# Routed experts: outputs turned by VectorE and scattered as quarters, inputs gathered as rows and passed through DRAM

## Chip, cores and metric

One core of one Trainium2 chip. The metric is the device time of one execution in microseconds; times below are of the kernel before the change.

## What is computed

```python
def reference(q, k, v, moe_w_group, moe_w_expert, moe_w1, moe_w2):
    x = attention(q, k, v)                   # [4608 tokens, 512]: local window plus 4x pooled attention
    g_logits = x @ w_group                   # 4 groups: argmax and its softmax value g_w
    for g in range(4):
        e_logits = x[mask_g] @ w_expert[g]   # 4 experts of the group: argmax and its softmax value e_w
        for e in range(4):
            h = np.maximum(xg[mask_e] @ w1[g, e], 0.0)     # 512 -> 1024
            ye = h @ w2[g, e]                              # 1024 -> 512
            out[tok_idx] = (g_w * e_w)[:, None] * ye
```

Everything is float32. Each of the 4608 tokens goes to one of 16 experts; its output row is the expert's result times the token's share g_w * e_w.

## The kernel before, in words

The first 230 us or so are attention: an order written out by hand (a string of steps, ORDER) over 16 units of two heads and two batches. Its results go to DRAM as rows of 512 floats, `xd` [4608, 512], written by `store_x` (line 455) in pieces of 512 B per row from the ACT queue. The router finds each token's expert and its share, and writes the shares to DRAM, 16 equal floats a token, `xw`, in `weight`. For each expert it makes a list of token numbers.

The experts follow. One expert is taken early and finished late, while attention still runs out; the other 15 are sorted by their count of tokens, and rank r has room for CAPS[r] of them (416, 384, 368, 352, ... 256, 256). Each rank r below 14 is one turn of `main`, that is one call of `ranked` (line 1157) with four experts: `pv`, the rank before, whose outputs are stored; `st`, the rank computed; `nx`, the next, whose weights are loaded and whose inputs are prepared; and `nn`, the one after, whose inputs are gathered. A turn stands in the program twice where the rank's count may be 20 smaller (`arm`): a branch picks one of the two.

A turn has ten steps. Steps 0 to 7 each compute a hidden block of 128 of the 1024 rows (`hidden`, line 961 the matmuls: 12 of C columns, since every float32 product is made of three float32r ones), then ScalarE takes the relu (line 965) and VectorE the rest that the rounding left (line 966). Steps 2 to 9 each project one hidden block into four accumulators (`project`, line 1012, 12 matmuls), which hold the output transposed: 128 of the 512 columns by C tokens. Weights come in four chunks (`weights_in`, line 876: 512 KB of w1 and 512 KB of w2, issued by SP into two raw buffers), and are split into a rounded part (ScalarE, line 881) and a rest (VectorE, line 882). A chunk waits until the one before the last is split and its raw buffer free. SP issues in order.

Outputs: at step 0 `drain` (line 1014) copies the four accumulators to `yt`, two by VectorE and two by ScalarE. At steps 1, 2 and 3 `store` (line 1025) turns one tile of 128 tokens with four transposes on TensorE (line 1034), scales it by the tokens' shares (ScalarE for even tiles, line 1039, VectorE for odd ones, line 1037) into `yo`, and GpSimd scatters the rows to `out` by an indirect DMA (line 1040). Ranks 1, 13 and 14 have a multiple of 128 tokens; they are computed in rows and have no drain and no turning.

Inputs of ranks 2 to 14: `xd` is read as quarters of a row, [4 * 4608, 128]. One indirect DMA of GpSimd gathers, for 32 tokens, quarter q to partitions 32q to 32q + 31 (`gather_quarters`, line 922, by `fetch`, line 905): with C tokens that is C / 32 of them per rank, spread over steps 1, 3, 5 and 7, the indices made by VectorE (`quarter_list`, line 826). Three more gather the shares. One turn later VectorE turns blocks of 32 by 32 (`turn_quarters`, line 935, steps 4 to 7), after which the columns stand in an order that the weights `w1q`, permuted on the host, have too; ScalarE and VectorE split them (lines 941, 942). Ranks 0 and 1 and the early and late expert gather rows instead and turn them on TensorE (`turn_in`, line 948).

Of the kernel before, what the change touches and what calls it, by code (L numbers as in the profile page):

```python
# [29 lines left out]
NTOK = B * S  # L30
LINE = 16
DM = H * D
# [13 lines left out]
SWITCHED = (0, *range(3, 13))  # L46

# [451 lines left out]
class Router:  # L499
# [7 lines left out]
    def __init__(self, ctx, tc, wg, we, cp, idf, xw):  # L507
        nc = self.nc = tc.nc
        self.idf, self.xw, self.cp = idf, xw, cp
# [142 lines left out]
    def weight(self, bp):  # L652
# [14 lines left out]
        nc.sync.dma_start(out=self.xw[G * P * bp : G * P * bp + G * P].rearrange("(g p) f -> p g f", p=P), in_=cw)  # L667
# [28 lines left out]
class Experts:  # L696
# [9 lines left out]
    def __init__(self, tc, cp, w1, w2, out, xd, xw, idf, R, ps, psd, px, lgp):  # L706
# [3 lines left out]
        self.w1, self.w2, self.out, self.xd, self.xw, self.idf = w1, w2, out, xd, xw, idf  # L710
# [29 lines left out]
        self.quad = f([P, 2], "quad")  # L740

    def numbers(self):
# [3 lines left out]
        for q in range(4):  # L746
            for i in range(2):
                nc.gpsimd.memset(self.quad[32 * q : 32 * q + 32, i : i + 1], float(q - 4 + 4 * i))
# [68 lines left out]
    def quarter_lists(self, c):  # L817

        n = NE - 3
        pt = self.psum([P, n, 4], "ql")  # L820
        self.nc.tensor.matmul(pt, self.four[:, c].rearrange("p q i -> p (q i)"), self.rv[:, 2 : n + 2], start=True, stop=True, skip_group_check=True)
        self.nc.vector.tensor_copy(self.qf[:, c], pt)

    def quarter_list(self, st, c):
        r = st["r"]
        self.nc.vector.tensor_scalar(
            out=self.qi[r % 2][:, c], in0=self.qf[:, c, r - 2], scalar1=self.quad[:, 0:1], scalar2=self.quad[:, 1:2], op0=ALU.add, op1=ALU.max
# [15 lines left out]
    def pools(self, ctx):  # L843
# [4 lines left out]
        self.xq = [xp.tile([P, 16, P], F32, name=f"xq{i}") for i in range(2)]  # L848
        self.qf = xp.tile([P, 4, NE - 3, 4], F32, name="qf")
        self.qi = [xp.tile([P, 4, 4], I32, name=f"qi{i}") for i in range(2)]  # L850
        self.four = xp.tile([P, 4, 4, 32], F32, name="four")
        self.xt = [xp.tile([P, 13, 32], F32, name=f"xt{i}") for i in range(2)]
        self.xs = [[xp.tile([P, 4, CAPS[i]], F32R, name=f"x{n}{i}") for n in "hl"] for i in range(2)]
        self.shares = [xp.tile([P, 4, LINE], F32, name=f"shares{i}") for i in range(4)]
        self.yt = xp.tile([P, 4, CAPS[0]], F32, name="yt")
# [28 lines left out]
    def gather(self, st, rows=NTOK):  # L884
# [4 lines left out]
        else:  # L889
            st["xh"] = self.xp.tile([P, 4, C], F32R, tag=n + "xh", name="xh")  # L890
            st["xl"] = self.xp.tile([P, 4, C], F32R, tag=n + "xl", name="xl")
            st["cw"] = self.xp.tile([P, C // P, LINE], F32, tag=n + "cw", name="cw")
        self.tiles(st)
        for t, (c, m, *_, w) in enumerate(st["xg"]):
            if "r" in st:
                xg = self.xq[st["r"] % 2].rearrange("p b c -> p (b c)")[:, DM * t : DM * t + DM]
            else:
                xg = self.xp.tile([P, DM], F32, tag=f"{n}xg{t}", name=f"xg{t}")
            self.fetch(xg[:w], self.xd[0:rows], st["gi"][:w, t : t + 1])
            st["xg"][t] = (c, m, xg, *st["xg"][t][3:])  # L900
        if "r" not in st:
            self.gather_shares(st, rows)

    def fetch(self, out, in_, index):
        self.nc.gpsimd.indirect_dma_start(  # L905
            out=out, out_offset=None, in_=in_, in_offset=bass.IndirectOffsetOnAxis(ap=index, axis=0), bounds_check=in_.shape[0] - 1, oob_is_err=False
        )

    def tiles(self, st):

        C = st["C"]
        cw = self.shares[st["r"] % 4] if "r" in st else st["cw"]
# [9 lines left out]
    def gather_quarters(self, st, blocks):  # L922

        C, r = st["C"], st["r"]
        if "xg" not in st:
            self.tiles(st)
# [651 lines left out]
```

## Time and profile before

| | us |
|---|---|
| median of 3 runs (693.62 to 693.8) | 693.62 |
| the profiled execution | 694.55 |
| its span, first to last instruction | 692.8 |
| TensorE busy in the span | 654.5 |
| VectorE, ScalarE, GpSimd busy | 486.7, 382.5, 427.1 |

The profile is of one execution; its span is 1.75 us shorter than that execution's own time, and that is 0.93 us above the median of the runs. TensorE's instructions overlap in the records, so the start of one matmul to the start of the next is what one costs in a stream, and the busy time of a group of them can be less than their number times the mean.

### The profile page before, as it was taken

The numbers are of one execution on the slowest core, as the hardware profiler recorded it, in microseconds if no ns is written. First come the engines' busy times: TensorE is split into PE (matmuls) and PEld (weight loads), VectorE is DVE, ScalarE is ACT, GpSimd is POOL, SyncE is SP. The second block draws the span as 40 slices with busy tenths as digits, with TensorE's granted clock in tenths as the row PEclk, the third lists the DMA queues.
The fourth block names the chain that finished last, engine by engine and source line by source line (L and its number), as shares of the span: only waits on it lengthen the run. The fifth ranks groups of instructions, "written<-read, shape, count | busy, mean of one in ns | idle before, by whom it ended". The sixth has DMA issues, their size and how long they took to land. (4 is left out here: it accounts for less than half of the span.)

```text
span 692.8 us, 18020 instructions
## 1 busy us (share of the span) xinstructions
PE 654.5 (94%) x6874; PEld 585.5 (85%) x6875; DVE 486.7 (70%) x937; ACT 382.5 (55%) x835; POOL 427.1 (62%) x457
## 2 busy tenths in 40 slices
PE   7798997998997999999999999999999999999996
PEld 4575775776765887999899999999999999999995
DVE  6987887988895686556456666667676767677751
ACT  8786765775773536344344454545555556556541
POOL 7957655668452745777564746667767677667411
PEclk9999999999999999999999999999999999999999
DMA  8798799889869537945464747677576686677720
GB/s 312 198 282 278 238 292 271 235 232 272 234 204 280 167 123 228 293 118 186 146 200 132 220 131 229 185 208 208 176 228 210 181 254 204 190 228 244 230 70 27
DMA packets 108450, 144.51 MB, mean 209 GB/s; under 512 B 25168, under 2 KB 77120, under 8 KB 108336
## 3 DMA queue, kind: packets, MB, share of 16 engines
q1 hardware_dynamic: 81120, 113.47, 54.2%
q0 software_dynamic: 9696, 20.72, 9.2%
q10 hardware_dynamic: 17520, 8.85, 4.6%
q8 instruction: 66, 1.08, 0.7%
q14 instruction: 48, 0.39, 0.2%
HBM read 121.47 MB, written 22.51 MB: 208 GB/s over the span
## 5 line engine op out<-in xcount | busy, mean ns | idle before, releaser
L905 POOL DMA_INDIRECT xq<-xd,qi x126 | 155.4, 1233 | 70.2 <-issue 36.9
L961 PE MATMUL ph<-xh,w1h 128*128 128x256 f32 (+13 forms) x512 | 153.9, 301 | 1.5 <-issue 1.0
L961 PE MATMUL ph<-xh,w1l 128*128 128x256 f32 (+13 forms) x512 | 152.3, 298 | 0.0
L961 PE MATMUL ph<-xl,w1h 128*128 128x256 f32 (+13 forms) x512 | 152.2, 298 | 0.0
L965 ACT ACTIVATE hh<-ph 128x256 fp32r<-128x256 f32 (+13 forms) x128 | 53.1, 416 | 172.7 <-PE ph L961 142.4
L966 DVE SCALAR_TENSOR_TENSOR hl<-ph,hh 128x256 fp32r<-128x256 f32 (+13 forms) x128 | 59.0, 463 | 99.3 <-ACT hh L965 64.3
L1012 PE MATMUL y<-hh,w2h 128*128 128x396 f32 (+11 forms) x384 | 117.4, 306 | 0.0
L1012 PE MATMUL y<-hl,w2h 128*128 128x396 f32 (+11 forms) x384 | 115.1, 300 | 0.0
L1012 PE MATMUL y<-hh,w2l 128*128 128x396 f32 (+11 forms) x384 | 115.0, 300 | 0.0
L1040 POOL DMA_INDIRECT out_dram<-yo,oi x47 | 57.9, 1231 | 79.2 <-ACT yo L1039 35.1
L961 PEld LDWEIGHTS ph<-xh,w1h 128*128 128x128 f32 x512 | 96.2, 188 | 3.3 <-issue 1.7
L961 PEld LDWEIGHTS ph<-xl,w1h 128*128 128x128 f32 x512 | 96.2, 188 | 0.9
L961 PEld LDWEIGHTS ph<-xh,w1l 128*128 128x128 f32 x512 | 96.2, 188 | 0.1
L882 DVE TENSOR_TENSOR w2l<-raww,w2h 128x1024 fp32r<-128x1024 f32 x61 | 74.4, 1222 | 22.5 <-ACT w2h L881 13.1
L882 DVE TENSOR_TENSOR w1l<-raww,w1h 128x1024 fp32r<-128x1024 f32 x61 | 74.4, 1219 | 13.2 <-ACT w1h L881 9.7
L1012 PEld LDWEIGHTS y<-hh,w2h 128*128 128x128 f32 x384 | 72.3, 188 | 0.6 <-DVE yo L1037 0.3
L1012 PEld LDWEIGHTS y<-hl,w2h 128*128 128x128 f32 x384 | 72.4, 189 | 0.1
L1012 PEld LDWEIGHTS y<-hh,w2l 128*128 128x128 f32 x384 | 72.3, 188 | 0.0
L881 ACT ACTIVATE w1h<-raww 128x1024 fp32r<-128x1024 f32 x64 | 67.5, 1055 | 4.1 <-DMA raww<-in_moe_w_dram 3.1
L881 ACT ACTIVATE w2h<-raww 128x1024 fp32r<-128x1024 f32 x64 | 67.2, 1051 | 1.2 <-DMA raww<-in_moe_w_dram 0.7
L905 POOL DMA_INDIRECT shares<-xw,gi x44 | 45.4, 1032 | 13.4 <-issue 13.4
L448 PE MATMUL b_x<-vw,pt 126*32 126x128 f32 x1152 | 39.9, 275 | 7.0 <-issue 3.7
(248 smaller groups left out, 1313.8 us busy)
## 6 DMA issues: line engine op xcount, KB each, us to landing
raww<-in_moe_w_dram SPq DMA_DIRECT2D x76, 512.0 KB
raww<-in_w1q_dram SPq DMA_DIRECT2D x52, 512.0 KB
vw<-in_vw_dram SPq DMA_DIRECT2D x32, 378.0 KB
kt<-in_k_dram SPq DMA_DIRECT2D x16, 576.0 KB
qT<-in_q_dram SPq DMA_DIRECT2D x16, 576.0 KB
xd<-x ACTq DMA_DIRECT2D x15, 576.0 KB
vs<-in_vm_dram SPq DMA_DIRECT2D x16, 512.0 KB
vw<-odd SPq DMA_DIRECT2D x16, 144.0 KB
```

Source lines behind the costliest of these rows:

```text
L448: self.nc.tensor.matmul(pt[32 * j : 32 * j + 32, t], self.of("pt", u)[:ROWS, 32 * lin : 32 * lin + 32], self.windows(u)[:ROWS, :, lin], st ...
L881: self.nc.scalar.activation(hi, raw, AF.Copy)
L882: eng.tensor_tensor(out=lo, in0=raw, in1=hi.bitcast(F32), op=ALU.subtract)
L905: self.nc.gpsimd.indirect_dma_start(out=out, out_offset=None, in_=in_, in_offset=bass.IndirectOffsetOnAxis(ap=index, axis=0), bounds_check ...
L961: nc.tensor.matmul(ph, a[:, k, cs], st[b][:, k, 0:C], start=(n == 0), stop=(n == 11))
L965: nc.scalar.activation(hh, ph, AF.Relu)
L966: nc.vector.scalar_tensor_tensor(out=hl, in0=ph, scalar=0.0, in1=hh.bitcast(F32), op0=ALU.max, op1=ALU.subtract)
L1012: nc.tensor.matmul(y, a[:, f % 2, cs], b, start=(f == 0 and n == 0), stop=(f == 7 and n == 2))
L1040: i = nc.gpsimd.indirect_dma_start(out=self.out, out_offset=bass.IndirectOffsetOnAxis(ap=oi, axis=0), in_=yo[:m], in_offset=None, bounds_c ...
```

## The change

- Turned ranks are 2 to 12 (`TURNED`). Their `drain` has no copies: VectorE transposes each accumulator in blocks of 32 by 32 straight into `yt` (two buffers), where 32 tokens by four quarters of a row then stand as 128 partitions of 128 floats. `store` is not called for them; at steps 1, 3, 5 and 8 VectorE makes the target indices of quarters, and `store_quarters` scatters up to three blocks, each by one indirect DMA of 128 pieces of 512 B. The order of columns that this needs comes from `w2q`, permuted on the host and read in place of w2.
- Since nothing scales the outputs any more, the inputs are scaled (relu and both products pass a factor through that is above zero). Rows in DRAM become 528 floats, the last 16 the share (`ROW`); `xw` and its gathers go. For rank `nn`, step 0 gathers whole rows (one indirect DMA per 128 tokens), steps 3, 4 and 5 scale a tile each on ScalarE, and at step 6 SP writes them to a DRAM buffer `xl` (two DMAs, `lay_down`). At step 0 of the next turn SP reads them back as quarters (four DMAs, `pick_up`) into one `xq`, where there were two.
- Ranks 0 and 1 and the early and late expert keep the shares of their gathered rows in a small tile (`keep_shares`, ScalarE) and scale at the end, as before. The last input tile of `turn_in` is 32, 64, 96 or 128 wide.

```diff
+ROW = DM + LINE
+TURNED = range(2, 13)
+SCATTER = (1, 3, 5, 8)
+SCALED = {3: (0,), 4: (1,), 5: (2,)}
...
     def targets(self, lo, hi, oi):
...
-        V.scalar_tensor_tensor(out=oi, in0=self.rv[:, lo:hi], scalar=-1.0, in1=self.none[:, lo:hi], op0=ALU.add, op1=ALU.add)
+        V.scalar_tensor_tensor(out=self.none[:, lo:hi], in0=self.rv[:, lo:hi], scalar=-1.0, in1=self.none[:, lo:hi], op0=ALU.add, op1=ALU.add)
+        V.tensor_copy(oi, self.none[:, lo:hi])
...
-        src2 = self.w2[ds(e, 1)].rearrange("a (k p) f -> p (a k) f", p=P)[:, 2 * c : 2 * c + 2, :]
+        src2 = self.w2[st.get("r", 0) in TURNED][ds(e, 1)].rearrange("a (k p) f -> p (a k) f", p=P)[:, 2 * c : 2 * c + 2, :]
...
+    def scale(self, st, t):
+        *_, xg, _, _, w = st["xg"][t]
+        self.nc.scalar.activation(xg[:w, 0:DM], xg[:w, 0:DM], AF.Copy, scale=xg[:w, DM : DM + 1])
+
+    def lay_down(self, st):
+
+        n = st["C"] // P
+        for t, m, w in ((0, n, P), (n, len(st["xg"]), st["xg"][-1][-1])):
+            if t < m:
+                self.nc.sync.dma_start(
+                    out=self.xl[st["r"] % 2].rearrange("(t p) c -> p t c", p=P)[:w, t:m], in_=self.xg[st["r"] % 2][:w, t:m, 0:DM]
+                )
+
+    def pick_up(self, st, q):
+        nb = (st["C"] + 31) // 32
+        self.nc.sync.dma_start(
+            out=self.xq[32 * q : 32 * q + 32, 0:nb], in_=self.xl[st["r"] % 2].rearrange("(b i) c -> i b c", i=32)[:, 0:nb, P * q : P * q + P]
+        )
...
     def drain(self, st):
...
+        if r in TURNED:
+            nb = (st["C"] + 31) // 32
+            yt = st["yt"] = self.yt[r % 2][:, 0 : 4 * P * 3].rearrange("p (b d j) -> p b d j", d=4, j=32)
+            for d in range(4):
+                nc.vector.transpose(yt[:, 0:nb, d], self.ys[d][:, 0 : 32 * nb].rearrange("p (b i) -> p b i", i=32))
+            return
...
+    def store_quarters(self, st, b):
+        t, c = divmod(b, 4)
+        if 32 * b < st["C"]:
+            self.scatter(self.out.rearrange("n (q c) -> (n q) c", q=4), self.qo[st["r"] % 2][:, c, t : t + 1], st["yt"][:, b].rearrange("p d j -> p (d j)"))
...
     def ranked(self, pv, st, nx, nn, hint):
...
                 self.drain(pv)
+                if st["r"] < 2:
+                    self.keep_shares(st)
                 if first:
                     self.gather(nx)
+                if nn:
+                    self.tiles(nn)
+                    for t in range(len(nn["xg"])):
+                        self.fetch(nn, t)
...
-            t = f if rows else f - 1
-            if t in range(len(pv["xg"])):
-                self.store(pv, t)
+            if turned:
+                if f in SCATTER:
+                    self.quarter_list(pv, SCATTER.index(f))
+                    for t in range(3):
+                        self.store_quarters(pv, 4 * t + SCATTER.index(f))
+            else:
+                t = f if rows else f - 1
+                if t in range(len(pv["xg"])):
+                    self.store(pv, t)
...
-            elif first and f in (2, 4):
-                self.gather_shares(st, lo=f - 2, hi=f)
-            elif first and f in (6, 8):
-                self.gather_shares(nx, lo=f - 6, hi=f - 4)
-            if nn and f in (1, 3, 5, 7):
-                self.quarter_list(nn, f // 2)
-                self.gather_quarters(nn, range(f // 2, 16, 4))
-            if nn and f == 8 + first:
-                self.gather_shares(nn)
             if f > 1:
                 self.project(st, f - 2)
+            for t in SCALED.get(f, ()):
+                if nn and t < len(nn["xg"]):
+                    self.scale(nn, t)
...
             if f in (1, 3, 5):
                 self.weights_in(nx, e, (f + 1) // 2)
+            if not first and f == 0:
+                for q in range(4):
+                    self.pick_up(nx, q)
+            if nn and f == 6:
+                self.lay_down(nn)
...
-    xd = dram.tile([NTOK, DM], F32, name="xd")
-    xw = dram.tile([NTOK, LINE], F32, name="xw")
+    xd = dram.tile([NTOK, ROW], F32, name="xd")
```

## Rows read from the trace of the kernel before

**Rows 1.** The page: busy time and share of the engines; TensorE in 40 slices.

```profile
PE 654.5 (94%) x6874; PEld 585.5 (85%) x6875; DVE 486.7 (70%) x937; ACT 382.5 (55%) x835; POOL 427.1 (62%) x457
...
PE   7798997998997999999999999999999999999996
```

**Rows 2.** TensorE's waits, 308 to 690 us: total, times, longest.

```profile
PE ph L961 <- issue: 1.0, 1, 1.0
PE ph L961 <- ACT yo L1039: 0.5, 1, 0.5
```

**Rows 3.** Windows: PE, PEld, DVE, ACT, POOL busy; clock; DMA share; GB/s.

```profile
437.02:464.85 27.83, 27.83 (x207) 27.80 (x205) 18.77 (x31) 14.39 (x24) 18.57 (x17) 1.00 0.67 200
...
618.14:641.16 23.02, 23.02 (x207) 22.96 (x205) 17.46 (x33) 13.72 (x25) 16.21 (x14) 1.00 0.72 219
...
100.00:125.00 25.00, 20.11 (x388) 14.60 (x387) 20.72 (x45) 15.08 (x50) 15.01 (x17) 1.00 0.96 287
```

**Rows 4.** TensorE's timeline around one store, turn of rank 5: start, duration.

```profile
437.02 0.30 PE L961 MATMUL ph<-xh,w1h 128*128 128x300 f32 x1
...
440.30 0.60 PE L1034 MATMUL yr<-idf,yt 128*128 128x128 f32 x4
440.66 0.39 PE L961 MATMUL ph<-xh,w1h 128*128 128x300 f32 x1
440.88 0.30 PE L961 MATMUL ph<-xl,w1h 128*128 128x300 f32 x1
441.01 0.30 PE L961 MATMUL ph<-xh,w1l 128*128 128x300 f32 x1
```

**Rows 5.** Instructions on the tiles yr and yt: ns min/median/max.

```profile
L1034 PE MATMUL yr<-idf,yt x148: 270/272/274, 313.0 to 649.3; 128*128 128x128 f32 x100, 128*32 128x128 f32 x8, 128*112 128x128 f32 x4, 128*96 128x128 f32 x4
L1039 ACT ACTIVATE yo<-yr,shares x24: 678/683/689, 314.2 to 650.2; 128x512 f32<-128x512 f32 x13, 112x512 f32<-112x512 f32 x1, 96x512 f32<-96x512 f32 x1, 80x512 f32<-80x512 f32 x1
L1037 DVE TENSOR_SCALAR yo<-yr,shares x13: 729/743/745, 317.5 to 648.9; 128x512 f32<-128x512 f32 x12, 32x512 f32<-32x512 f32 x1
...
L1023 ACT ACTIVATE yt<-y x24: 391/428/517, 307.4 to 641.0; 128x416 f32<-128x416 f32 x2, 128x368 f32<-128x368 f32 x2, 128x352 f32<-128x352 f32 x2, 128x336 f32<-128x336 f32 x2
L1021 DVE COPY yt<-y x24: 416/479/592, 307.9 to 641.8; 128x416 f32<-128x416 f32 x2, 128x368 f32<-128x368 f32 x2, 128x352 f32<-128x352 f32 x2, 128x336 f32<-128x336 f32 x2
```

**Rows 6.** Instructions on the tile xt: ns min/median/max.

```profile
L941 ACT ACTIVATE xh<-xt x68: 272/442/548, 223.4 to 664.1; 128x256 fp32r<-128x256 f32 x12, 128x128 fp32r<-128x128 f32 x4, 128x416 fp32r<-128x416 f32 x4, 128x384 fp32r<-128x384 f32 x4
...
L935 DVE STREAM_TRANSPOSE xt<-xq x52: 434/500/575, 326.6 to 663.3; 128x320 f32<-128x320 f32 x16, 128x288 f32<-128x288 f32 x16, 128x352 f32<-128x352 f32 x8, 128x256 f32<-128x256 f32 x8
```

**Rows 7.** The page's costliest groups: busy, mean ns, idle before.

```profile
L905 POOL DMA_INDIRECT xq<-xd,qi x126 | 155.4, 1233 | 70.2 <-issue 36.9
...
L1040 POOL DMA_INDIRECT out_dram<-yo,oi x47 | 57.9, 1231 | 79.2 <-ACT yo L1039 35.1
...
L881 ACT ACTIVATE w1h<-raww 128x1024 fp32r<-128x1024 f32 x64 | 67.5, 1055 | 4.1 <-DMA raww<-in_moe_w_dram 3.1
```

**Rows 8.** SP's timeline, turn of rank 5: start, duration.

```profile
442.16 0.37 SPq L876 DMA_DIRECT2D raww<-in_w1q_dram  x1
```

**Rows 9.** Waits of SP, 300 to 690 us: total, times, longest.

```profile
SPq L876 <- DVE hl L966: 97.8, 32, 7.6
```

**Rows 10.** Windows of 1 us after that issue; columns as in rows 3.

```profile
442.20:443.20 1.00, 1.00 (x10) 1.00 (x9) 0.69 (x3) 1.00 (x3) 0.89 (x1) 1.00 0.00 0
...
444.20:445.20 1.00, 1.00 (x10) 1.00 (x9) 1.00 (x4) 0.04 (x1) 0.95 (x1) 1.00 1.07 340
```

**Rows 11.** ScalarE's timeline, turn of rank 5: start, duration.

```profile
450.40 1.05 ACT L881 ACTIVATE w1h<-raww 128x1024 fp32r<-128x1024 f32 x1
```

**Rows 12.** DMA queues in the turn of rank 12: packets, MB, share.

```profile
q1 hardware_dynamic: 2923, 3.93, 57.0%
q0 software_dynamic: 512, 1.05, 13.8%
```

**Rows 13.** The page: the ACT queue of DMAs over the span.

```profile
q10 hardware_dynamic: 17520, 8.85, 4.6%
```

More of the change, by code (lines that the diff above doesn't have):

```diff
@@ L30 @@
 NTOK = B * S
+DM = H * D
 LINE = 16
-DM = H * D
+ROW = DM + LINE
 F = 1024
@@ L746, in numbers @@
         for q in range(4):
-            for i in range(2):
-                nc.gpsimd.memset(self.quad[32 * q : 32 * q + 32, i : i + 1], float(q - 4 + 4 * i))
+            nc.gpsimd.memset(self.quad[32 * q : 32 * q + 32], float(q))
         for r, c in enumerate(CAPS):
@@ L817, in quarter_lists @@
     def quarter_lists(self, c):
-        n = NE - 3
-        pt = self.psum([P, n, 4], "ql")
-        self.nc.tensor.matmul(pt, self.four[:, c].rearrange("p q i -> p (q i)"), self.rv[:, 2 : n + 2], start=True, stop=True, skip_group_check=True)
+        lo, hi = TURNED.start, TURNED.stop
+        pt = self.psum([P, hi - lo, 3], "ql")
+        self.nc.tensor.matmul(pt, self.four[:, c].rearrange("p q i -> p (q i)"), self.none[:, lo:hi, 0:3], start=True, stop=True, skip_group_check=True)
         self.nc.vector.tensor_copy(self.qf[:, c], pt)
@@ L826, in quarter_list @@
         self.nc.vector.tensor_scalar(
-            out=self.qi[r % 2][:, c], in0=self.qf[:, c, r - 2], scalar1=self.quad[:, 0:1], scalar2=self.quad[:, 1:2], op0=ALU.add, op1=ALU.max
+            out=self.qo[r % 2][:, c], in0=self.qf[:, c, r - TURNED.start], scalar1=self.quad, scalar2=None, op0=ALU.add
         )
@@ L891, in gather @@
             st["xl"] = self.xp.tile([P, 4, C], F32R, tag=n + "xl", name="xl")
-            st["cw"] = self.xp.tile([P, C // P, LINE], F32, tag=n + "cw", name="cw")
+            st["tiles"] = self.xp.tile([P, C // P, ROW], F32, tag=n + "xg", name="xg")
         self.tiles(st)
[L894 to L907, printed above, removed]
+        for t in range(len(st["xg"])):
+            self.fetch(st, t, rows)
     def tiles(self, st):
-        C = st["C"]
-        cw = self.shares[st["r"] % 4] if "r" in st else st["cw"]
+        C, r = st["C"], st.get("r")
+        xg = st["tiles"] if r is None else self.xg[r % 2]
         st["xg"] = []
@@ L915, in tiles @@
             m = min(P, C - P * t)
-            st["xg"].append((P * t, m, None, st["oi"][:m, t : t + 1], cw[:, t], P if m <= P // 2 else m))
-    def gather_shares(self, st, rows=NTOK, lo=0, hi=4):
-        for t, (*_, cw, _) in list(enumerate(st["xg"]))[lo:hi]:
-            self.fetch(cw, self.xw[0:rows], st["gi"][:, t : t + 1])
[L922 to L926, printed above, removed]
-        for b in blocks:
-            t, c = divmod(b, 4)
-            if 32 * b < C:
-                self.fetch(self.xq[r % 2][:, b], self.xd.rearrange("n (q c) -> (n q) c", q=4), self.qi[r % 2][:, c, t : t + 1])
+            share = None if r is not None and r > 1 else self.shares(st)[:m, t : t + 1]
@@ new lines, in tiles, with fetch, shares @@
+            st["xg"].append((P * t, m, xg[:, t], st["oi"][:m, t : t + 1], share, 32 * ((m + 31) // 32)))
+    def fetch(self, st, t, rows=NTOK):
+        *_, xg, _, _, w = st["xg"][t]
+        self.nc.gpsimd.indirect_dma_start(
+            out=xg[:w], out_offset=None, in_=self.xd[0:rows], in_offset=bass.IndirectOffsetOnAxis(ap=st["gi"][:w, t : t + 1], axis=0),
+            bounds_check=rows - 1, oob_is_err=False,
+        )
+    def shares(self, st):
+        i = st.get("r", 2 + (st["C"] == P))
+        return self.share[:, 4 * i : 4 * i + 4]
@@ L949, in turn_in @@
         self.split(st["xh"][:, k], st["xl"][:, k], pt[:, : st["C"]])
+        if k == 3 and "r" not in st:
+            self.keep_shares(st)
     def hidden(self, st, f):
@@ L1287, in tables @@
     def tables(self, dram):
+        self.xl = [dram.tile([3 * P, DM], F32, name=f"xl{i}") for i in range(2)]
         self.t_units = dram.tile([UNITS, 2], I32, name="t_units")
```

63 lines of the change are left out of this document (38 added, 25 removed).

## The prediction

> **What bounds the kernel now.** I read the page first: TensorE is busy 94% of the span, and its slices stand at 9 from the fourteenth to the last but one; beside its own weight loads, which overlap, no other engine is above 70% [rows 1]. That says which engine, not which stage, and a busy TensorE need not be one that gains from less work. So I read its waits from the first rank's store to the end: two, 1.5 us in all, in 380 us [rows 2]. Nothing is late for TensorE there; whatever leaves its instruction stream shortens the run until something else becomes late. The windows by turn say how far off that is: in the turn of rank 5 (437.02 to 464.85) VectorE has 18.77 of 27.83 us busy, ScalarE 14.39, GpSimd 18.57, the DMA engines 0.67; in the turn of rank 12 (618.14 to 641.16), one of the shortest, 17.46, 13.72 and 16.21 of 23.02 us, DMA 0.72 [rows 3]. The attention stage before 230 us is another case: from 100 to 125 us the DMA share is 0.96 and TensorE is busy 20.11 of 25 us [rows 3].
>
> **What leaves TensorE.** A store of ranks 0 and 2 to 12 turns four 128-column blocks on TensorE. The timeline of one store shows the price: 24 matmuls of the hidden layer start between 437.02 and 440.30, 0.137 apart; at 440.30 the four transposes start where the 25th would have; that matmul begins at 440.66, its successor at 440.88, the third at 441.01 [rows 4]. Undisturbed the third would have begun at 440.57, so a store displaces 0.44 us. The instruction's own 272 ns would say 1.09 for four, since their ends overlap; the shift of what follows is what the end of the run sees. The trace has 148 such transposes [rows 5]: 12 ranks, 16 of rank 0 (four tiles), and 11 times 12 of ranks 2 to 12. These 132 go: 33 stores by 0.44 is **14.5 us**. Bounds: 0.36 for the four starts alone gives 11.9, and 0.46 with one more disturbed start gives 15.2. Smaller: the last tile of rank 0's input is turned 32 wide instead of 128, 4 instructions by at most 0.09, so 0 to 0.4 us; I take 0.2.
>
> **What VectorE gets.** Per turned rank two copies of 0.479 and one scaling of 0.743 go [rows 5], and four transposes of 32 by 32 blocks come, from PSUM. Nearest row: the same instruction from SBUF, median 0.50 [rows 6]; the copy from PSUM, 0.479, is no dearer, so I take 0.50 and bound it by 0.45 and 1.0. That is 2.0 for 1.7, so 17.8 of about 21.7 us busy in the turn of rank 12: covered. The place matters more: all four stand at the head of the turn, ahead of the first relu residue, and the accumulators they empty are needed by the first projection, three hidden blocks later (36 matmuls: 4.9 us at the 0.137 of 300 columns [rows 4], 4.0 at the 244 of rank 12). Each starts as its quarter of the last projection ends, so they are done 1 to 1.5 us into the turn; even at 1.0 each they are done by 3.3. Nothing is late. The index arithmetic (one small operation at four steps) stays, at steps 1, 3, 5, 8 instead of 1, 3, 5, 7.
>
> The Trainium skill speaks against this part: its page "VectorE: DVE Perf Modes", section "Rules for kernel authors", gives a 128 by 128 transpose to TensorE when PSUM will do as the destination. By that rule the 33 stores would stay and the time with them, near 693.6; the rows say that here it is TensorE that has no time left, and the sum goes by them.
>
> **ScalarE.** Two drains (0.428) and two scalings (0.683) go per turned rank [rows 5], 2.2 us; three scalings of the gathered rows come for ranks 2 to 14. Between the 0.683 from PSUM and half of the 1.055 for 1024 columns from SBUF [rows 7] I take 0.6, so 1.8. The tightest step is 5: relu and input split, near 0.44 each [rows 6], scaling 0.6 and weight split 1.05 are 2.5 of the 2.7 us that a hidden block and a projection take at rank 12; covered, and steps 8 and 9 have little.
>
> **GpSimd.** Ten gathers of quarters (1.233), three of shares and three scatters (1.231) per rank [rows 7] become three row gathers and ten quarter scatters. With as many indices each, I price them alike, at 1.25 and a quarter between two: 16 issues become 13, 19.5 us instead of 24, in turns of 21 to 34. The tightest cover of the change is here. Behind the two or three scatters of step 8, which wait for VectorE's index operation, stand the next turn's row gathers: with 1 us for that wait, the first is issued 5.5 us after step 8 began, 2.8 us into the next turn, and with 2.5 us to land (an estimate: the weight chunk below, twice as large, takes about 3) is there at 5.3; ScalarE reads it behind the relu of step 3, at 6.8 or later. Each further tile comes 1.5 us later and is read a step of 2.7 us later. No cost; without that 1.5 us, ScalarE's relu is late next.
>
> **The DRAM trip: SP and the DMA engines.** Two DMAs lay a rank's rows down and four pick them up, six more issues of 0.37 on SP [rows 8], 2.2 us a turn; SP now waits 97.8 us for VectorE's relu residues alone, behind which the weight buffers come free [rows 9], and that idle time hides them. Order on SP: weight chunk 3, lay-down (waits for the scaling of step 5), next chunk 0 (freed at steps 6 and 7), the pick-ups (wait for the lay-down to land and for the last turning of step 7), chunk 1. Half a chunk, 512 KB, issued at 442.16 [rows 8] moves nothing until 443.2, then up to 340 GB/s [rows 10]: some 3 us to land. The lay-down has steps 6 and 7, 5.4 us or more, before the pick-ups are reached. Behind them chunk 1 is queued: issued at 442.16, first read by ScalarE at 450.40 [rows 11], 5 us to spare. The picked-up blocks are turned at step 4, some 13 us after. Cost 0 with that cover; without it, the first thing late is chunk 1.
>
> The engines' own time: in the turn of rank 12 the 3.93 MB of the hardware queue take 57.0% of 23.02 us, 13.1 us, so 3.34 us per MB; the indirect queue 13.8%, 3.2 [rows 12]. Lay-down and pick-up of 256 rows of 2 KB are 1.05 MB more, 3.5 us; the share gathers that go, and 64 B per row that come, nearly cancel. So 16.6 becomes 20.1 of 21.6 us, share **0.93**, under the 0.96 that the attention stage held for 25 us [rows 3]; at rank 5 18.6 becomes 22.8 of 26.5, 0.86. I take 0 and bound it at 6 us (below).
>
> **Attention stage.** The rows in DRAM are 2112 B apart, not 2048, under the same 512 B writes; the ACT queue's time is 4.6% of the span, 32 us [rows 13]. No row shows the new pitch: a fifth dearer is 6 us of DMA time among 230, of which at most 1.5 would show. I take 0.3. The shares of the early and late expert come with their rows, three gathers fewer on GpSimd, with no TensorE wait behind them: 0 to 0.5 back, taken as 0.
>
> **Sum.** The profiled execution took 694.55 (span 692.8 and 1.75 around it), the median of the runs is 693.62, 0.93 lower. 694.55 - 14.5 - 0.2 + 0.3 = 680.15; less 0.93, **679.2**.
>
> **Rivals.**
> A, the forecast: the turns of ranks 3 to 13 shrink by 1.3 us each and TensorE still waits for nothing. For it: two waits in 380 us, and every cover above is 1.5 us or more. 676.5 to 681.
>
> B, the DMA engines become the bound in the late turns. For: 0.93 by the sum, in a stream that arrives in bursts, with 4 us more of engine time in a turn that is 1.3 shorter. Against: at a share of 1.07 they moved 340 GB/s [rows 10], and turn 12 needs 3.93, 1.05 and 1.05 MB in 21.6 us, 279 GB/s. If a share of 0.9 is all that bursts allow, the turns of ranks 8 to 13 take 22.3 instead of 21.7, 0.6 to 1 us each: 3.6 to 6, so 683 to 685. The Trainium skill bears on this: "DMA: Bandwidth & Descriptors", section "Rules for kernel authors", wants at least 1 MiB per DMA and calls anything under 64 KB mostly overhead. The pick-ups are 128 to 176 KB each, between the two; at twice the price per byte they would add 1.8 us to the 20.1, which is this rival. No row here shows such a DMA.
>
> C, slower than before: the pick-ups hold SP. They wait in SP's queue for a write to DRAM to be confirmed, and chunk 1 stands behind them. It decides once that wait lasts beyond about 10 us into a turn (5 us of spare at chunk 1, 5 more in the relu that waits behind it on ScalarE); each microsecond beyond stalls TensorE by one, in 13 turns. To lose all that is gained takes 14.4 / 13 = 1.1 us per turn; at 2 us it is 705. For: two trips in one queue are new here. Against: 3 us landings seen, and a lay-down issued some 9 us before the turn begins.
>
> D, hidden anyway: something unseen paces the turns at their old length, 693 to 694. For: SP spends most of the time waiting for VectorE [rows 9], so the weight stream moves at VectorE's pace. Against: the turns are as long as their matmuls and stores: 192 by 0.137 and three by 0.44 are 27.6, of the 27.83 that rank 5 took.
>
> **Chances.** A 0.73, B 0.16, C 0.07, D 0.04. Faster by over 0.2% (1.4 us, about what a measurement of this kernel can tell from no change) takes A and B, 0.89; D is the same, 0.04; C is slower, 0.07. The range holds A and most of B: 676 to 686; it leaves C and D out.
>
> **What would show it.** Right: 16 transposes from line store, none in ranks 2 to 12; the turn of rank 12 at 21.7 us and that of rank 5 at 26.5; TensorE waits from 300 us on still about 1.5 us; block transposes from PSUM near 0.50; DMA share 0.85 to 0.95 late. Wrong by B: late turns longer than 192 matmuls, weight splits waiting for a weight DMA. Wrong by C: SP waiting for the lay-down past the start of a turn, the same splits late from rank 1 on. Wrong by the attention term: the gaps of TensorE before 230 us grow by more than 1 us.

## The result, and the profile after

The changed kernel takes 684.82 us (median, 683.76 to 686.88), the kernel before beside it 693.62: a ratio of 0.988, interval 0.985 to 0.991. That is faster, inside the range, and 5.6 us above the predicted 679.2. Two later series of the unedited kernel, both on the chip that the record numbers 2, gave 0.990 (0.986 to 0.993) and 0.998 (0.994 to 1.002), more below.

From the page of the changed kernel, its span, busy times and DMA queues (packets, MB, share of 16 engines):

```profile
span 683.7 us, 17694 instructions
PE 642.7 (94%) x6743; PEld 573.8 (84%) x6743; DVE 489.3 (72%) x942; ACT 384.5 (56%) x833; POOL 353.7 (52%) x394
...
q1 hardware_dynamic: 102496, 129.99, 65.7%
q0 software_dynamic: 7952, 20.47, 10.1%
q10 hardware_dynamic: 17520, 8.85, 4.8%
q8 instruction: 66, 1.08, 0.7%
```

The span fell by 9.1 us. TensorE has 11.8 us less work than in [rows 1], so it is idle longer than before, the reverse of what was forecast. GpSimd lost 73 us, which moved nothing by itself. Queue q8, which the prediction did not read, brings instructions: 66 packets of 16 KB.

Now the same kernel's TensorE waits from 300 us to 690 us, which answer to [rows 2]:

```profile
PE ph L979 <- issue: 3.4, 4, 1.3
PE y L1030 <- issue: 0.5, 1, 0.5
```

Before, 1.5 us in two waits; now 3.9 in five. None names an engine or a DMA: "issue" is time in which TensorE waited for nothing that the profile shows. Three of the five stand at the start of a turn, the other two, 0.54 each, inside the turns of ranks 10 and 12.

Third, the windows of the turns of ranks 5 and 12 (length, busy us of PE, PEld, DVE, ACT, POOL, clock, DMA share, GB/s), to set against [rows 3]:

```profile
434.40:461.00 26.60, 26.60 (x195) 26.60 (x193) 18.77 (x33) 14.43 (x23) 17.11 (x15) 1.00 0.95 260
610.62:633.19 22.57, 22.03 (x195) 21.85 (x194) 16.98 (x33) 13.25 (x22) 13.42 (x12) 1.00 0.94 266
```

Rank 5 came out as forecast (26.5), with a DMA share of 0.95 and TensorE never idle. Rank 12 is 0.9 over its 21.7, half a microsecond of it idle. So a full DMA share is not what costs, and the late turns are where the time stayed. Turn lengths, from the start of one turn's first matmul of the hidden layer to the next one's; the last column is a version that comes up below:

| turn of rank | before | after | after, code moved by 8 KB |
|---|---|---|---|
| 4 | 29.18 | 27.74 | 28.40 |
| 5 | 27.83 | 26.59 | 26.59 |
| 6 | 26.86 | 25.72 | 25.72 |
| 8 | 25.60 | 25.83 | 24.39 |
| 10 | 24.45 | 25.39 | 23.05 |
| 12 | 23.02 | 22.57 | 21.78 |
| 3 to 13 | 286.65 | 276.95 | 272.02 |

Early turns lost 1.1 to 1.4 us, where 1.3 was forecast; those of ranks 8 and 10 grew. The timeline of TensorE at the end of turn 8 shows how (start, us, then what; the bracket is the idle time before):

```profile
536.59 0.29 PE L1030 MATMUL y<-hl,w2h 128*128 128x276 f32 x1
536.72 0.28 PE L1030 MATMUL y<-hh,w2l 128*128 128x276 f32 x1
538.15 0.39 PE L979 MATMUL ph<-xh,w1h 128*128 128x268 f32 x1 [1.15 <-issue]
```

Within a turn one matmul follows the other after 0.13 us; here, between two turns, 1.43 passed. What stands there in the program is the branch that picks the arm of the next turn (line 1178). That line's view, from 505 us on, gives for TensorE's sequencer (min/median/max in ns, first and last start):

```profile
L1178 PEldq COMPARE_BRANCH  x5: 1605/2535/3323, 509.9 to 608.7; - x5
```

The five branches that end the turns of ranks 7 to 11 took 1.6 to 3.3 us; the five before them 0.33 to 0.35. The sequencer runs ahead of the matmuls (at 534.8 it reaches the branch that the matmuls reach at 536.85), so of 3.3 us some 1.3 show. What is late can be seen in the DMA view of 534.8 to 538.1, the time of that branch:

```profile
q8 instruction: 1, 0.02, 1.7%
```

A piece of code was being fetched (535.7 to 536.6). At the branch at 458.7, which took 0.33, the view of 458.7 to 460.4 has no line of q8. All 14 profiles of this document show the same: from 300 us on, 93 branches took 0.36 us or less, and at none was a q8 packet on its way; 40 took 1.0 us or more, and at 38 of them one was, at the other two (1.0 and 1.5 us) one had landed up to 0.4 us before. From a long branch to the next branch three or four packets came, from a short one mostly two.

The kernel before had one long branch that it paid for:

```profile
L1147 PEldq COMPARE_BRANCH  x5: 328/344/3572, 373.8 to 489.5; - x5
```

Its 3.57 us, at 404.2, is the "issue" wait of 1.0 us in [rows 2].

**The account.** Turns 3 to 13 lost 9.70 us. Six starts that came late cost 4.9 us in them (start to start, less the usual 0.13), against 1.8 for two before; without these, 12.8. Turn 0 began 0.44 later, turn 2 took 0.28 longer and all the rest 0.13 less. That makes the 9.1 of the span.

### The profile page after: what moved, and what is told of

It is laid out like the page before. It is cut to its first block, busy times and chain, and to the rows that moved or that the text cites. A ratio compares the mean times of both kernels' runs of the same rounds, so it can differ in the third digit from the quotient of the medians.

```text
span 683.7 us, 17694 instructions
## 1 busy us (share of the span) xinstructions
PE 642.7 (94%) x6743; PEld 573.8 (84%) x6743; DVE 489.3 (72%) x942; ACT 384.5 (56%) x833; POOL 353.7 (52%) x394
## 3 DMA queue, kind: packets, MB, share of 16 engines
q1 hardware_dynamic: 102496, 129.99, 65.7%
## 5 line engine op out<-in xcount | busy, mean ns | idle before, releaser
L1072 POOL DMA_INDIRECT out_dram<-yt,qo x110 | 130.2, 1184 | 133.2 <-DVE qo L831 107.9
L1030 PE MATMUL y<-hh,w2h 128*128 128x396 f32 (+11 forms) x384 | 115.9, 302 | 0.0
L914 POOL DMA_INDIRECT xg<-xd,gi x47 | 53.2, 1132 | 54.9 <-ACT share L927 25.9
L1072 POOL DMA_INDIRECT out_dram<-yo,oi x14 | 15.9, 1134 | 53.5 <-ACT yo L1063 20.6
L452 PE MATMUL b_x<-vw,pt 126*32 126x128 f32 x1152 | 38.0, 275 | 3.9 <-DMA vw<-odd 2.4
```

The lines of the kernel that those rows point to most:

```text
L452: self.nc.tensor.matmul(pt[32 * j : 32 * j + 32, t], self.of("pt", u)[:ROWS, 32 * lin : 32 * lin + 32], self.windows(u)[:ROWS, :, lin], st ...
L914: self.nc.gpsimd.indirect_dma_start(out=xg[:w], out_offset=None, in_=self.xd[0:rows], in_offset=bass.IndirectOffsetOnAxis(ap=st["gi"][:w, ...
L1030: nc.tensor.matmul(y, a[:, f % 2, cs], b, start=(f == 0 and n == 0), stop=(f == 7 and n == 2))
L1072: i = self.nc.gpsimd.indirect_dma_start(out=out, out_offset=bass.IndirectOffsetOnAxis(ap=index, axis=0), in_=y, in_offset=None, bounds_che ...
```

## Experiments: is it the load?

Theory L: the DMA engines, at 0.94 and more, deliver TensorE's code late. Rival theories blame the lost transposes' price (D), SP (C), or the code itself. Four kernels, beside each other on one chip.

**A sixth of the trip's bytes**, in the changed kernel:

```diff
-                    out=self.xl[st["r"] % 2].rearrange("(t p) c -> p t c", p=P)[:w, t:m], in_=self.xg[st["r"] % 2][:w, t:m, 0:DM]
+                    out=self.xl[st["r"] % 2].rearrange("(t p) c -> p t c", p=P)[:32, t : t + 1], in_=self.xg[st["r"] % 2][:32, t : t + 1, 0:DM]
...
-        nb = (st["C"] + 31) // 32
+        nb = 1
```

> The changed kernel, with the trip through DRAM cut to a sixth of its bytes: the same six DMAs a turn, but the lay-down writes 32 rows per DMA and each pick-up reads one block of 32 tokens; xq is cleared once. It leaves out most of the experts' inputs of ranks 2 to 14. TensorE's program is the same, instruction for instruction. Theory load (DMA engines at 0.94 to 0.98 delay the fetching of TensorE's instructions): the DMA share of the late turns falls to 0.75 to 0.80, the branches that end the turns of ranks 7 to 11 take about 0.35 us instead of 1.6 to 3.3, TensorE's waits from 300 us on fall from 3.9 us to 2 or less, and the run takes 680 to 681.5. Rival layout (where the shorter turns put the branch among the fetched blocks decides, whatever the load): the same branches stay at 1.6 to 3.3 us and the run at 684 to 685.

Measured: 686.35 us, ratio 0.984 (0.980 to 0.989). Its windows of turns 5, 9 and 12, columns as above:

```profile
434.83:461.42 26.59, 26.59 (x194) 26.59 (x193) 18.67 (x33) 14.08 (x23) 16.73 (x15) 1.00 0.69 214
541.15:566.71 25.56, 24.14 (x193) 23.93 (x193) 17.53 (x33) 13.63 (x23) 14.48 (x13) 1.00 0.70 211
614.47:636.24 21.77, 21.77 (x194) 21.77 (x193) 16.34 (x32) 12.95 (x22) 11.78 (x12) 1.00 0.74 236
```

Its line on the hardware queue, from the page, which is needed further below, and then its branches from 505 us on:

```profile
q1 hardware_dynamic: 84768, 115.90, 55.1%
```

```profile
L1179 PEldq COMPARE_BRANCH  x5: 425/2254/4412, 510.4 to 612.6; - x5
```

The share (last but one number) fell to 0.7, and the branches stayed long: turn 9 has 1.4 us of idle TensorE with a third of the DMA engines' time free. A full DMA system does not decide whether a branch is long. The time lies between the two forecasts and decides nothing.

A long branch can cost more than its wait. In this kernel TensorE waited 2.17 us at the end of turn 7; soon after, its granted clock fell to the lower of its two levels, 1.2 of 2.4 GHz. Here is that stretch, and one of the same length behind the wait of 1.67 us at that place in a later profile of the unedited kernel:

```profile
515.90:519.30 3.40, 3.40 (x17) 3.40 (x16) 1.18 (x2) 1.34 (x2) 1.93 (x2) 0.50 0.70 205
514.30:517.70 3.40, 3.40 (x27) 3.40 (x28) 0.61 (x2) 1.35 (x2) 2.57 (x3) 1.00 1.10 327
```

Turn 8 has no wait inside and took 26.33 us, where 24.39 will do (table above). Three more of the kernels below (without DRAM, hint at step 6, shift by 16 KB) have such a fall right behind their wait of 2.7 to 3.7 us at the end of turn 7; a wait of 2.54 us in the unedited kernel has none. In no other turn of ranks 3 to 13 of any profile was the clock below 1.00.

**The transposes alone**, taken out of the kernel before, which has no trip:

```diff
+            if st["r"] > 1:
+                y = self.yt.rearrange("p d c -> p (d c)")[:, DM * t : DM * t + DM]
+            else:
...
```

> The kernel before, with the four transposes of a store left out for ranks 2 to 12: the tile is scaled straight from the drained copy, so its columns are not the output's. No trip through DRAM, no quarter scatters. TensorE's program in the turns is as short as in the changed kernel, the DMA load is that of before. It measures the term of 14.5 us alone. Theory load: 679 (678 to 680.5), branches of 0.35 us but for the one or two that the kernel before has too. Rival layout: waits at the late branches as in the changed kernel, 682 to 683.5. Third theory, the term itself is smaller (0.39 a store, 12.9 in all): 680.7 with clean branches.

Measured: 685.91 us, ratio 0.986 (0.980 to 0.991), as much as the whole change. Its branches from 505 us on:

```profile
L1150 PEldq COMPARE_BRANCH  x5: 343/2254/3432, 513.6 to 612.7; - x5
```

The last four, at 538.8, 564.3, 587.7 and 612.7, took 3.43, 2.25, 2.67 and 1.69 us. So neither the trip nor the scatters bring them: fewer TensorE instructions do.

**The trip alone**, added to the kernel before (six DMAs a turn of the same sizes, at the same steps, into buffers that nothing reads):

```diff
+            if not first and f == 0:
+                for q in range(4):
+                    self.pick_up(nx, q)
+            if nn and f == 6:
+                self.lay_down(nn)
```

> The kernel before, plus the six DMAs of the trip in every turn, at the same places of SP's queue and of the same size, between DRAM and a tile that nothing else uses. Nothing is left out. TensorE's program is that of before. Theory load: DMA share 0.85 to 0.95 in the late turns, more branches over 1 us, and 696 to 698. Rival layout: 693.6 within 1 us, branches as before. If SP's queue were what costs (the weights behind the pick-ups), ScalarE would wait for weight DMAs in every turn and the run would be above 700.

Measured: 702.15 us, ratio 1.010 (1.006 to 1.014). Its branches, up to 505 us and from there on:

```profile
L1163 PEldq COMPARE_BRANCH  x5: 328/344/4172, 376.5 to 492.9; - x5
L1163 PEldq COMPARE_BRANCH  x5: 328/333/3783, 519.6 to 625.8; - x5
```

The two branches that were the longest before (3.57 and 1.0 us, at 404.2 and 542.0) are long, 4.17 and 3.78, and no other is. Load makes no new long branch; whether it lengthens one is not shown, since in the unedited changed kernel the same branch, at the end of turn 7, took 2.3, 4.6 and 3.9 us in three profiles. There the trip costs 7.5 us on 694.65: more than the changed kernel lost, and not all of it stands in TensorE's waits, so the price of the trip depends on what else runs and was not settled.

**Without DRAM**: 16 DMAs from SBUF to SBUF in the place of the pick-ups.

```diff
-                for q in range(4):
-                    self.pick_up(nx, q)
-            if nn and f == 6:
-                self.lay_down(nn)
+                self.across(nx)
```

> The changed kernel without DRAM between: 16 DMAs a turn from the gathered rows in SBUF straight to the quarters in SBUF, 32 partitions each, at the place of the pick-ups. The whole result is computed. Half of the trip's bytes go, ten issues of 0.37 on SP come. Theory load: DMA share near 0.85 to 0.90 late, fewer waits at branches, 681.5 to 683.5, under the changed kernel. Rival layout: 684 to 685 with the same branches. If SP is then late with weight chunk 1, the splits wait for its DMA and it is above 686.

Measured: 701.97 us, ratio 1.011 (1.006 to 1.015). SP's timeline in its turn of rank 12, which begins at 619.02:

```profile
619.54 0.38 SPq L881 DMA_DIRECT2D raww<-in_moe_w_dram  x1
620.02 11.69 SPq L939 DMA_DIRECT2D xq<-xg  x16
632.07 0.28 SPq L881 DMA_DIRECT2D raww<-in_w1q_dram  x1
```

And, from its view of tile w1h from 300 us on, what ended the idle time before the splits of w1 (us, times):

```profile
  DMA raww<-in_w1q_dram: 20.2, 11
```

This is rival C at work, in another kernel: 16 issues hold SP for 11.7 us, weight chunk 1 goes out 13.0 us into the turn, and the turn takes 25.71 us instead of 22.57. In the changed kernel the pick-ups at the end of turn 8 look like this:

```profile
535.58 0.38 SPq L881 DMA_DIRECT2D raww<-in_w2q_dram  x1
536.44 2.15 SPq L944 DMA_DIRECT2D xq<-xl  x4
542.64 0.40 SPq L881 DMA_DIRECT2D raww<-in_w1q_dram  x1
```

Four issues in 2.15 us, the last one out 0.4 us after turn 9 began at 538.15; chunk 1 follows 4.5 us into it.

## Experiments: where the code lies, or where its hint stands?

Theory E: the code that the hint at step 2 fetches is displaced by the turn's own code before the branch. Theory P: what decides is where a turn's code lies within the 16 KB pieces of q8. The changed kernel runs beside them as it is.

> The changed kernel, unedited, as the mate of the runs beside it. Both theories expect the ratio to the kernel before that its first run gave, 0.988 (0.985 to 0.991), and the branches that end the turns of ranks 8 to 12 long again, at the same places (2.3, 3.3, 2.5, 3.3 and 1.6 us in its first profile, where the others take 0.33 to 0.35).

Measured: 683.96 us, ratio 0.990 (0.986 to 0.993); the same five branches are long, 1.5 to 4.6 us (those that end the turns of ranks 7 to 11; the expectation counts the ranks one too high). Their places came back, their lengths did not; in a third profile, below, three of the five are long.

**The hint at step 6** (in the changed kernel, and in the kernel before without its transposes):

```diff
-            if f == 2 and hint:
+            if f == 6 and hint:
```

> The changed kernel with one edit: TensorE's hint of the next turn's code stands at step 6 of a turn and not at step 2. Theory E (the hinted code is fetched, but the code that the turn itself runs through next displaces it before the branch): at step 6 at most one such stretch follows, so the long branches go, 0.35 us each, TensorE's waits with the releaser issue from 300 us on fall from about 4 us to under 2, and it is 3 to 4 us faster than the changed kernel, ratio to before about 0.983. Theory L (the fetch is late because the DMA engines are full, at a share of 0.93 and more): a hint given later leaves it less time, so the long branches stay or grow, and the ratio is 0.988 or higher.

> The kernel before without the 132 transposes of ranks 2 to 12 (their yt is not turned, so those output rows hold other numbers; everything else is done) and with the hint at step 6. Its mate with the hint at step 2 gave a ratio of 0.9855, with four long branches. Theory E: they go, and the ratio shows what the transposes alone are worth, 12.9 to 14.5 us, so 0.979 to 0.982. Theory L: the DMA engines are no fuller here than in the kernel before, and its long branches were four all the same; the hint's place would change nothing, 0.985 to 0.986. Theory D (something else sets the pace, and the transposes are worth only 9 us): 0.986 with no long branch left.

Measured: 685.79 us, ratio 0.993 (0.990 to 0.995), and 685.02, ratio 0.988 (0.984 to 0.992). The branches of the first:

```profile
L1178 PEldq COMPARE_BRANCH  x5: 1437/3412/4357, 510.4 to 612.7; - x5
```

All five as long as before, and in the second three are 2.0 to 3.3 us: theory E falls. The late hint does make the queue fetch: 71 packets of q8 in each of the two, where their mates with the hint at step 2 have 66 and 65. The second did not show what the transposes alone are worth either.

**Code moved by 8 KB**: 64 small transposes, whose result nothing reads, ahead of the turns. Each is a matmul and a weight load, 128 instructions in all, half of the 256 that make 16 KiB by the Trainium skill's page "Runtime: NRT & Kernel Launch", section "Instruction fetch mechanics" (the shifts below agree).

```diff
     def choice(self):
+        pt = self.psum([32, 32], "pad")
+        for _ in range(64):
+            self.nc.tensor.transpose(pt, self.idf[:32, :32], self.idf[:32, :32])
```

> The changed kernel with 64 small transposes on TensorE ahead of the turns, whose result nothing reads: they cost some 4 us or less once, and move all code of the turns by 4 to 8 KB. Theory E (which turn misses is set by where its code lies): the long branches stand at other turns than those that end ranks 8 to 12, while the DMA share of each turn stays. Theory L (full DMA engines): the same turns have the long branches. Time: the changed kernel's and up to 4 us more, give or take the 3 us that long branches are worth.

Measured: 682.57 us, ratio 0.988 (0.986 to 0.991), the 2.0 us of the 64 transposes paid. Its branches from 505 us on:

```profile
L1181 PEldq COMPARE_BRANCH  x5: 328/333/358, 511.6 to 606.6; - x5
```

And all of TensorE's waits from 300 us on:

```profile
PE y L1030 <- DVE hl L984: 0.7, 2, 0.5
```

Not one long branch in the late turns, and no "issue" wait left. The DMA load did not change: the same 129.99 MB. One branch far ahead did become long, as theory E expected of some: the one before the turn of rank 0 took 3.85 us, against 0.58 to 1.05 in the unedited kernel; the wait behind it was 0.2 us.

**By 8 and by 16 KB, at the start**: the 12 idle matmuls of 512 columns at the kernel's begin become 76 of 80, or 140 of 44.

```diff
-        for i in range(n):
-            self.nc.tensor.matmul(pt, self.warm[:, 0:P], self.warm, start=True, stop=True)
+        m, w = (76, 80) if n == 12 else (n, 4 * P)
+        for i in range(m):
+            self.nc.tensor.matmul(pt[:, 0:w], self.warm[:, 0:P], self.warm[:, 0:w], start=True, stop=True)
```

> The changed kernel, unedited, beside the two shifted ones. Long branches (2 us and more) at the ends of the turns of ranks 7 to 10 and a shorter one, 1.5 us, at rank 11's, as in both profiles so far; ratio to before 0.988 to 0.990.

> The changed kernel whose first 12 idle matmuls of 512 columns, which run while TensorE waits for the first loads, are 76 of 80 columns: 128 TensorE instructions more, 8 KB of code, at no time. Theory P (where a turn's code lies in the 16 KB pieces that the instruction queue fetches decides whether its branch is long): no long branch from 300 us on, as with the 64 transposes that cost 2.0 us, turns of ranks 7 to 10 at 25.4, 24.4, 23.9 and 23.1 us, waits with the releaser issue under 1 us, and 3 to 4 us less than the changed kernel: a ratio to before of 0.982 to 0.985. Theory L (full DMA engines make the fetch late): the same turns long, ratio 0.988 to 0.990.

> As the 8 KB shift, with 140 idle matmuls of 44 columns: 256 instructions, 16 KB, one whole piece. Theory P: the code lies in its piece as in the changed kernel, so the long branches are back at the ends of ranks 7 to 11 and the time is the changed kernel's, ratio 0.988 to 0.990. If the 8 KB shift helped for another reason (fewer or more instructions ahead, the start), this one helps as well, ratio 0.982 to 0.985.

Measured in this series: 688.56 us for the changed kernel (0.998, 0.994 to 1.002), 687.12 with 8 KB (0.995, 0.992 to 0.998), 688.58 with 16 KB (0.999, 0.995 to 1.002). The branches with 8 KB and with 16 KB:

```profile
L1179 PEldq COMPARE_BRANCH  x5: 328/333/358, 517.9 to 615.8; - x5
```

```profile
L1179 PEldq COMPARE_BRANCH  x5: 425/2703/5795, 516.6 to 619.8; - x5
```

Gone at half a piece, back at a whole one (the unedited kernel had three of 3.1 to 3.9 us in this series, the 16 KB one four): theory P holds for the branches. The times did not follow. One reason is that "at no time" was wrong. The 8 KB kernel's timeline at the start has this:

```profile
12.85 2.06 PE L325 MATMUL b_d<-kd,qd 64*128 64x144 f32 x16 [4.00 <-issue]
```

In the 16 KB kernel TensorE waits 1.8 us in that stretch for the same nothing; without the extra instructions 1.9 us at most, for VectorE. So not all of the 4.0 is new: the next idle matmuls begin at 14.84 and 14.07, against 12.40 and 13.19 in two profiles of the unedited kernel. The two profiles are of runs 5.7 and 6.9 us above their kernels' medians, so the size is rough.

**By 8 KB, in a wait**: the 64 transposes where TensorE waits for the early expert's second gather.

```diff
         for c, _, xg, _, _, w in st["xg"]:
+            if "r" not in st and k == 0 and c == P:
+                for _ in range(64):
+                    self.nc.tensor.transpose(pt[:32, P : P + 32], self.idf[:32, :32], self.idf[:32, :32])
```

> The changed kernel with 64 small transposes, whose result nothing reads, where TensorE waits 0.8 to 3.3 us for the second gather of the early expert (at about 221 us in the profiles so far): 8 KB of code, for 2.0 us of TensorE of which at least a part lies in that wait. Theory P: no branch over 0.5 us from 300 to 620 us, waits with the releaser issue under 1 us in 380 us, turns of ranks 7 to 10 at 25.4, 24.4, 23.9 and 23.1 us as in the first 8 KB shift, ranks 3 to 13 together 273 to 275 us (286.65 in the kernel before, 277 to 281 in the changed one). Time 2 to 4 us under the changed kernel's on the same chip; as its ratio to before was 0.988, 0.990 and 0.998 on three chips, that is 0.983 to 0.994. Theory L: long branches at the ends of ranks 7 to 11 as in the unedited kernel, and its ratio or up to 2 us above it.

Measured: 680.2 us (676.23 to 682.27), the kernel before beside it 692.29: ratio 0.982 (0.977 to 0.986). Its branches from 505 us on:

```profile
L1181 PEldq COMPARE_BRANCH  x5: 328/333/358, 509.8 to 603.8; - x5
```

All of TensorE's waits from 300 us on:

```profile
PE ph L982 <- issue: 0.4, 1, 0.4
PE y L1033 <- ACT yo L1066: 0.2, 1, 0.2
```

And the windows of turns 5, 9 and 12:

```profile
434.25:460.84 26.59, 26.59 (x194) 26.59 (x193) 18.85 (x33) 14.20 (x23) 16.17 (x15) 1.00 0.88 256
536.30:560.19 23.89, 23.89 (x194) 23.89 (x193) 17.90 (x33) 13.99 (x23) 15.22 (x14) 1.00 0.96 273
605.66:627.44 21.78, 21.78 (x194) 21.78 (x193) 16.40 (x32) 13.23 (x22) 12.49 (x12) 1.00 0.97 281
```

This is the changed kernel as it was forecast: TensorE waits for 0.6 us, and turn 12 takes 21.78 us against 21.7. The time is 1 us above the 679.2, or 1.7 when the ratio is put on the 693.62 of the first series. It has the lowest ratio of all the kernels tried, though the unedited one did not run beside it. The turns of ranks 7 to 10 took 25.35, 24.39, 23.89 and 23.05 us, as expected before it ran. Turn 4 is 0.7 longer than in the unedited kernel (table above), with an "issue" wait of 0.4 in its middle: such waits move with the code as well. Its DMA share in turn 12 is 0.97, and with 0.74, in the kernel with a sixth of the trip, the turn took 21.77. The DMA engines set nothing here.

**What stays open.** The kernel before was profiled once, beside the first result, so why its distance to the changed kernel was 1.2%, 1.0% and 0.2% in three series was not found (the last two were on one chip, not on two as the expectation above has it). The lengths of the long branches, which change from run to run, are one candidate. The granted clock is another: runs of one kernel with a lower mean clock tend to take longer (of the kernel before, 688.81 us at 0.990 and 694.96 at 0.984 in one series), and in the series at 0.2% the changed kernel had 0.985 on average and the kernel before 0.990, in the one at 1.0% 0.986 and 0.988. Why a branch whose target was hinted is long in some places of the code, the runs do not tell.

## Why the prediction was right, and where its number was off

**TensorE's 14.5 us.** The term is the right one, and a little large. In the version without long branches turns 3 to 13 lost 14.63 us, 1.2 of it because starts that came late cost 1.8 before and 0.6 now: 13.4, or 0.41 us a store where 0.44 was taken from one store's timeline [rows 4]; in the changed kernel itself 12.8, or 0.39. Both lie inside the bounds, 11.9 to 15.2. The 16 transposes that were to stay are the ones that stayed, as the changed kernel's view of tile yt shows (min/median/max in ns, first and last start, forms):

```profile
L1041 DVE STREAM_TRANSPOSE yt<-y x44: 439/476/583, 376.0 to 633.8; 128x320 f32<-128x320 f32 x16, 128x288 f32<-128x288 f32 x16, 128x352 f32<-128x352 f32 x8, 128x384 f32<-128x384 f32 x4
L1058 PE MATMUL yr<-idf,yt x16: 270/272/273, 313.4 to 325.5; 128*128 128x128 f32 x12, 128*32 128x128 f32 x4
```

**The step that failed** is forecast A's "TensorE still waits for nothing", and behind it the sentence that whatever leaves its stream shortens the run "until something else becomes late". The prediction looked among the engines and DMAs for what could be late; it was TensorE's own code. It priced 33 stores as time on TensorE, and not as 24 instructions less in a turn's code (12 matmuls and their weight loads), by which all that lies behind them moves. That gave 3.1 us back. The view that would have shown it was at hand: the "issue" wait of [rows 2] was read as a small number, not as a question. The trace of before had its answer, a branch of 3.57 us, where eight of the other nine after 300 us took 0.33 to 0.35.

The Trainium skill has the rule that was missing, in the section named above: code comes in blocks of 16 KiB, fetched ahead in sequence, and a taken branch to a block that is not there stalls until it has come. The runs agree with the block and the stall: a shift by 128 instructions cleared the late branches, one by 256 brought them back, each q8 packet is 16 KB, and one was on its way at 38 of the 40 long branches and at none of the 93 short ones. They put a price on the stall, 1.0 to 5.8 us in the sequencer.

**What it comes to.** 679.2, and 3.1 for late starts, 1.7 for the smaller store, 0.4 for what lies ahead of turn 3 (0.7 instead of the 0.3 of the attention term), 0.2 for the rank 0 tile, of which nothing was seen: 684.6, against 684.82. The 0.4 is not resolved: turn 3 of the unedited kernel began at 377.3, 375.3 and 377.7 us in three profiles (376.6 before), and TensorE's gaps before 230 us, whose growth by 1 us was to speak against that term, were 29.7, 27.3 and 24.4 (28.2 before).

So the time lies above the 676.5 to 681 of forecast A, and inside the stated range only because that range also held most of rival B, whose mechanism did not come. That part of being right was luck.

**VectorE, ScalarE, GpSimd: free, as said.** The block transposes from PSUM took 0.476 us (0.50 taken); VectorE is busy 16.98 us of turn 12 (17.8 forecast). By the rule of the Trainium skill's "VectorE: DVE Perf Modes", section "Rules for kernel authors", the time would have stayed; it fell, since what counted was TensorE's time. The scaling of a row tile and a scatter of quarters took 0.715 and 0.985 us (0.6 and 1.25 taken), and neither shows. From the view of tile xg:

```profile
L931 ACT ACTIVATE xg<-xg x37: 706/715/727, 286.3 to 622.2; 128x512 f32<-128x512 f32 x27, 64x512 f32<-64x512 f32 x4, 32x512 f32<-32x512 f32 x4, 96x512 f32<-96x512 f32 x2
```

And from that of tile yt:

```profile
L1072 POOL DMA_INDIRECT out_dram<-yt,qo x110: 977/985/1988, 382.9 to 657.5; - x110
```

**Rival B, the DMA engines.** The share came out as forecast (0.93; measured 0.94, and 0.97 in the shorter turn), rank 5's higher (0.86 against 0.95). That rival would have given 683 to 685, which the result hit for another reason: its sign, weight splits waiting for a weight DMA, amounts to 1.2 us in four waits from 300 us on, none of which TensorE felt, and turns at 0.95 to 0.97 have no gap. The trip is dearer than the 3.34 us per MB taken for it. The sixth of the trip moved 14.1 MB less and freed 65.7% of 683.7 less 55.1% of 686.8 us, 70.8 us: 5.0 us per MB, a part of which is other packets that became faster. By their own packets the pick-ups, in pieces of 512 B, take 5.2 us of engine time per MB; the lay-downs, in pieces of 2 KB, stay near the 3.3 of the rest of the queue. The Trainium skill's "DMA: Bandwidth & Descriptors", section "Rules for kernel authors", ties the rate to the size of a DMA; here pick-ups (128 to 176 KB) and lay-downs (64 to 512 KB) differ in their pieces as well, and no run separates the two. All of it is hidden.

**Rival C** did not come: SP waited 6.4 us in all for lay-downs. Its mechanism is real and near, as the 16 issues showed; their 13.0 us into the turn, 3 beyond the 10 from which it was to decide, lengthened turn 12 by 3.1. **Rival D** falls with the turns of ranks 3 to 6.

## What to carry to other kernels

When TensorE is full and a program branches, an edit that removes TensorE instructions also moves code; look at the branch instructions of its sequencer, before and after, before explaining a missing gain by load or waits. An "issue" wait between two arms of a branch is such a place, and a few idle instructions in a wait that exists anyway can move the code off it: here the turns of ranks 3 to 13 then took 272.0 us instead of 277.0. And a DMA share near 1 is no bound by itself: ask for the wait that names the transfer.

## What was not expected of the hardware

- From 300 us on, a TensorE branch took 0.33 us (0.64 at most) or 1.0 to 5.8 us. Which of the two changed with a shift of the code by 8 KB and came back with one by 16 KB; neither a sixth of the trip's load nor the hint's place changed it.
- Behind a wait of 2.2 to 3.7 us at such a branch the granted clock fell from 1.00 to 0.50 in four profiles; behind one of 2.5 us it stayed at 1.00. In one of the four the turn of rank 8 took 1.9 us more than without the fall.
- With 128 more instructions ahead of the first loads TensorE had 4.0 us of "issue" wait within the first 13 us in one profile, with 256 1.8 us in another; the work behind came 0.9 to 2.4 us later.
- Sixteen SBUF to SBUF DMAs kept SP for 11.69 us, 0.73 each, twice the 0.37 of a weight load's issue [rows 8].
